# Turning the keys of groups 0 and 1 on TensorE, and query group 0 behind the last values of batch 0

## The chip, the cores and the metric

The kernel runs on one core of one Trainium2 chip. The metric is the time on the device in microseconds (us), median over runs; lower is better. TensorE (PE in the profile) multiplies matrices and writes to PSUM; VectorE (DVE), ScalarE (ACT) and GpSimd (POOL) work on tiles; SyncE (SP) issues most of the transfers.

## The reference, cut to what matters

Agent attention over four batches, followed by a feed-forward layer that takes the maximum of three products:

```python
# q, k, v: (4, 12544, 128); agents: (4, 49, 128)
def sm(a, b):                                   # softmax of scaled scores
    s = scale * (a @ b.transpose(0, 2, 1))
    s = s - s.max(-1, keepdims=True)
    e = np.exp(s)
    return e / (e.sum(-1, keepdims=True) + 1e-09)
agent_v = sm(agents, k) @ v                     # (4, 49, 128): all keys of a batch
x = (sm(q, agents) @ agent_v).reshape(50176, 128)
h = np.maximum(np.maximum(x @ w1, x @ w2), x @ w3)   # (50176, 768)
out = h @ w_out                                 # (50176, 128)
```

`agent_v` of a batch needs every key and value of that batch, and no query of the batch can be finished before it is there.

## The kernel before: the parts concerned

The kernel first goes through all keys and values of batch 0 (12 groups, called "early"). Then 49 query groups of 1024 rows follow. While the query groups of one batch are worked on, the keys and values of the next batch are taken along, one key group `s` of up to 1152 rows with each query group `s`. Instructions are not issued where they are written: each step is put in a list with a key, and the list is emitted in order of the keys. A step with a lower key stands earlier on its engine.

Matmuls contract over partitions, so keys and queries must first be turned (transposed) so that their 128 features lie on partitions. There are two ways in the kernel for this: on TensorE against an identity, into PSUM, with a copy to SBUF behind it, or by a DMA that transposes from SBUF to SBUF.

```python
def k_group(b, t0, n, key, s):          # n blocks of 128 keys; s is None for batch 0
    early = s is None
    ...
    def cast_k():                       # fp32 -> bf16 on GpSimd
        d["kb"] = work.tile([P, KT, C], BF16, tag="k_bf", bufs=3, name="k_bf")
        nc.gpsimd.tensor_copy(out=d["kb"][:, :n, :], in_=d["k"][:, :n, :])

    def turn_k():
        d["kT"] = work.tile([P, KT, P], BF16, tag="kT", bufs=3, name="kT")
        if early or s == 0:
            t = d["kT_ps"] = uv_tile(BF16).rearrange("p i c -> p (i c)")
            for j in range(n):
                nc.tensor.transpose(t[:, j * P:(j + 1) * P], d["kb"][:, j, :], ident)
        else:
            nc.sync.dma_start_transpose(out=d["kT"][:, :n, :],
                                        in_=d["kb"][:, :n, :].rearrange("p j c -> p (j c)"))

    def evacuate():
        nc.vector.tensor_copy(out=d["kT"][:, :n, :].rearrange("p j c -> p (j c)"),
                              in_=d["kT_ps"][:, :n * P])

    def scores(): ...                   # L255: kT x agents
    def exps(): ...                     # L260: e_k, on ScalarE
    def values(): ...                   # L266: v x e_k (and L269: sums, in batch 0)
    def add_values(): ...               # L276: into Vacc, on VectorE
```

`uv_tile` gives one of three PSUM buffers, which the hidden matmuls of the feed-forward layer use as well; whoever takes one waits until its last user of three takes ago is read out.

Once batch 0's values are summed, `k_tail` normalises them (`avT`) and multiplies them into the weights, which gives `G`, the product of the agents' values with the first layer, in two halves. The early version is cut here to its core:

```python
def product(c0, c1, on_vector):
    t = uv_tile()
    ...                                          # L352: avT x wall
    if on_vector:
        nc.vector.tensor_copy(out=G[b][:, c0:c1], in_=src)
    else:
        nc.scalar.activation(G[b][:, c0:c1], src, AF.Copy)
...
for i, (c0, c1) in enumerate(((C31, WC), (C21, C31))):    # 1024 and 768 columns
    on_vector = s is None and i == 1
```

A query group is turned (L415), copied (L419), scored (L429) and exponentiated (L435). Then come six pairs of hidden matmuls (L455): each first half `u` gets a ReLU on ScalarE (L470; the fourth goes L467, L478), each second half `v` is taken to the maximum with it on VectorE (L480). The output matmuls are L485 and L494, the scaling of the output L501. `keep_busy` (L200) and `fill` (L577) are matmuls whose results are not used; they keep TensorE occupied.

```python
if s == 0:
    at(last_key - 29.9, load)
    at(last_key - 3.5, cast)
    at(last_key + 0.63, turn_q, ("qt", 0), (), "om", [("qe", 0)])
    at(last_key + 0.635, evacuate, ("qe", 0), [("qt", 0)])
    at(last_key + 0.82, scores, ("s", 0), [("qe", 0)], "om", [("ex", 0)])
    at(last_key + 0.825, exps, ("ex", 0), [("s", 0)])
```

Of the kernel before, what the change touches and what calls it, by code (L numbers as in the profile page):

```python
# [11 lines left out]
AF = mybir.ActivationFunctionType  # L12
# [4 lines left out]
def kernel(  # L17
# [18 lines left out]
    nc = tc.nc  # L36
# [53 lines left out]
    def at(key, fn, name=None, needs=(), ring=None, frees=()):  # L90

        ops.append((key, len(ops), fn, name, needs, ring, frees))
# [115 lines left out]
    def k_group(b, t0, n, key, s):  # L210

        d = {}
        early = s is None

        def load():
            for name, src in (("k", k), ("v", v)):
                t = d[name] = load_tile()
                nc.sync.dma_start(t[:, :n, :], src[b, t0 * P:(t0 + n) * P, :].rearrange(
                    "(p j) c -> p j c", j=n))

        def cast_k():
            d["kb"] = work.tile([P, KT, C], BF16, tag="k_bf", bufs=3, name="k_bf")
            nc.gpsimd.tensor_copy(out=d["kb"][:, :n, :], in_=d["k"][:, :n, :])  # L223

        def cast_v():
            d["vb"] = work.tile([P, KT, C], BF16, tag="v_bf", bufs=4, name="v_bf")
            if early:
                nc.scalar.activation(d["vb"][:, :n, :], d["v"][:, :n, :], AF.Copy)  # L228
            else:
                nc.gpsimd.tensor_copy(out=d["vb"][:, :n, :], in_=d["v"][:, :n, :])  # L230

        def turn_k():
            d["kT"] = work.tile([P, KT, P], BF16, tag="kT", bufs=3, name="kT")
            if early or s == 0:
                t = d["kT_ps"] = uv_tile(BF16).rearrange("p i c -> p (i c)")
                for j in range(n):
                    nc.tensor.transpose(t[:, j * P:(j + 1) * P], d["kb"][:, j, :], ident)  # L237
# [8 lines that stand above are left out]
        def scores():  # L246
            if early:
                d["pair"] = uv_tile()
                d["s"] = d["pair"][:, 0, :]
                last_tile["t"] = d["s"]  # L250
            else:
                d["s"] = host[s]
            t = d["s"]
            for j in range(n):
                nc.tensor.matmul(t[:, j * A:(j + 1) * A], d["kT"][:, j, :], agT[:, b, :A],  # L255
                                 start=(j == 0), stop=True, skip_group_check=True)

        def exps():
            d["e"] = work.tile([P, KT * A], BF16, tag="e_k", bufs=3, name="e_k")
            nc.scalar.activation(d["e"][:, :n * A], d["s"][:, :n * A], AF.Exp, scale=scale)  # L260

        def values():
            t, c = (d["pair"][:, 1, :], 0) if early else (d["s"], CV)
            for j in range(n):
                e = d["e"][:, j * A:(j + 1) * A]
                nc.tensor.matmul(t[:, c:c + A], d["vb"][:, j, :], e, start=(early and j == 0),  # L266
                                 stop=True, skip_group_check=True)
                if early:
                    nc.tensor.matmul(t[:, A:2 * A], ones_bf, e, start=False, stop=True,  # L269
                                     skip_group_check=True)  # L270

        def add_values():
            w = 2 * A if early else A
            src = d["pair"][:, 1, :w] if early else d["s"][:, CV:CV + A]
            if t0:
                nc.vector.tensor_tensor(out=Vacc[b], in0=src, in1=Vacc[b], op=ALU.add)  # L276
            else:
                Vacc[b] = work.tile([P, w], FP32, tag=f"Vacc{w}", name="Vacc")
                nc.vector.tensor_copy(out=Vacc[b], in_=src)

        def add_exps():
            if t0:
                nc.gpsimd.tensor_tensor(out=Eacc[b][:, :n * A], in0=Eacc[b][:, :n * A],  # L283
                                        in1=d["e"][:, :n * A], op=ALU.add)
            else:
                Eacc[b] = work.tile([P, KT * A], FP32, tag="Eacc", name="Eacc")
                nc.gpsimd.tensor_copy(out=Eacc[b], in_=d["e"])

        if early:
            g = ("early", t0)  # L290
            at(key - 30, load)
            at(key - 5, cast_k)
            at(key - 4, cast_v)
            at(key, turn_k, ("kt", g), (), "uv", [("kt_out", g)])
            at(key + 0.5, evacuate, ("kt_out", g), [("kt", g)])

            last = [("normalise", 0)] if t0 + n == NT else []
            late = max(0, (key - last_key) / 6 + 2)
            at(min(key + 6.6, last_key + 0.58 + 0.02 * late), scores, ("ks", g), [("kt_out", g)],
               "uv", [("ka", g)] + last)  # L300
            at(min(key + 7, last_key + 0.64 + 0.01 * late), exps, ("ke", g), [("ks", g)])
            done = last_key + (0.6 + 0.1 * late if late >= 1 else 0.55)
            at(min(key + 13.2, done), values, ("kv", g), [("ke", g)])
            at(min(key + 13.6, done + 0.01), add_values, ("ka", g), [("kv", g)])
        else:
            at(key + KEY["ks"] - 22, load)
            at(max(key + KEY["ks"] - 10, last_key - 3.4), cast_k)
            at(max(key + KEY["ks"] - 8, last_key - 3.3), cast_v)
            if s:
                at(max(key + KEY["ks"] - 6.5, last_key - 3.2), turn_k, ("kt_out", s))  # L310
            else:
                at(last_key + 1.05, turn_k, ("kt", s), (), "uv", [("kt_out", s)])
                at(last_key + 1.06, evacuate, ("kt_out", s), [("kt", s)])

            at(key + KEY["ks"] if s else KEY["u0"] + 0.6, scores, ("ks", s), [("kt_out", s), ("ho", s)])
            at(key + KEY["ke"], exps, ("ke", s), [("ks", s)])
            at(key + KEY["ke"] + 1.5, add_exps, ("kx", s), [("ke", s)])
            at(key + KEY["kv"], values, ("kv", s), [("ke", s)])
            at(key + KEY["ka"], add_values, ("ka", s), [("kv", s)])

    def k_tail(b, sum_key, keys, s):
        d = {}
# [41 lines left out]
        at(sum_key + (0.9 if s is None else 0.01), normalise, ("normalise", b),  # L364
           [("ka", ("early", NT - last_size)) if s is None else ("total", s)])
        for i, (c0, c1) in enumerate(((C31, WC), (C21, C31))):
            on_vector = s is None and i == 1
            at(keys[i], lambda c0=c0, c1=c1, on_vector=on_vector: product(c0, c1, on_vector),
               ("product", b, i), [("normalise", b)], "uv", [("product", b, i)])

# [12 lines left out]
    def q_group(s):  # L383
        pairs = [range(0, 2), range(2, 4)]
        n, nh = GT, GT // 2
        parts = split(s * GT, (s + 1) * GT, 2)
        key = 6.0 * s
        d = {}
# [27 lines left out]

        def evacuate():
            d["qT"] = work.tile([P, GT, P], BF16, tag="qT", bufs=3, name="qT")
            nc.vector.tensor_copy(out=d["qT"].rearrange("p j c -> p (j c)"), in_=d["qT_ps"])  # L419

        def turn_q_dma():
            d["qT"] = work.tile([P, GT, P], BF16, tag="qT", bufs=3, name="qT")
# [95 lines left out]
        if s == 0:  # L518
            at(last_key - 29.9, load)
            at(last_key - 3.5, cast)  # L520
            at(last_key + 0.63, turn_q, ("qt", 0), (), "om", [("qe", 0)])
            at(last_key + 0.635, evacuate, ("qe", 0), [("qt", 0)])
            at(last_key + 0.82, scores, ("s", 0), [("qe", 0)], "om", [("ex", 0)])
            at(last_key + 0.825, exps, ("ex", 0), [("s", 0)])
        elif s < SB:
            at(key + K["qt"] - 20, load)
            at(max(key + K["qt"] - 7, last_key - 3), cast)
            put("qt", turn_q, ring="om", frees=[("qe", s)])
            put("qe", evacuate, ("qt", s), *([("s", s - 3)] if s >= 3 else []))
        else:  # L530
            at(key + K["s"] - 24, load)
            at(key + K["s"] - 8, cast)
            at(key + K["s"] - 5.5, turn_q_dma, ("qe", s))
# [48 lines left out]
    last_key = KEY["u0"] - 2  # L582
# [7 lines left out]
    fillers = []  # L590
    for g, n in enumerate(first_sizes):
        k_group(0, sum(first_sizes[:g]), n, first_key + 6.0 * g, None)

        if 4 <= g < len(first_sizes) - 5:
            fillers += [(first_key + 6.0 * g + 0.55, 3), (first_key + 6.0 * g + 1.3, 3)]
    k_tail(0, last_key, (last_key + 0.95, last_key + 0.96), None)
    for key, n in fillers + [(last_key + 0.9, 2), (last_key + 1.1, 3)]:
        at(key, lambda n=n: keep_busy(n), ("busy", key), (), "om", [("busy", key)])
    tails = {b * NT // GT: b for b in range(1, B)}
    hosting = set()  # L600
# [44 lines left out]
```

The softmax here doesn't subtract the row's maximum and nothing guards it: scores larger than these inputs give would overflow.

## Time and profile before

| what | before |
|---|---|
| time, median of 3 runs | 473.62 us (472.06 to 474.02) |
| span of the profiled execution | 473.2 us |
| TensorE busy | 439.0 us (93%) |
| VectorE busy | 408.1 us (86%) |
| ScalarE busy | 395.9 us (84%) |
| GpSimd busy | 166.1 us (35%) |
| mean granted TensorE clock | 0.991 |
| transfers | 118.04 MB, mean 249 GB/s |

Busy time says how full an engine is over the whole span; it does not say which engine another one waits for in a given stretch. For that there are the chain of work that ended last, which is followed back from the last instruction, the waits, and the timeline with the idle time ahead of each instruction and the instruction that ended it. Stretches of the span can be tabled one by one with each engine's busy time, the granted TensorE clock as a share of full speed, and the busy share of the 16 DMA engines. Matmuls overlap in time, so their busy time in a table of stretches is not the same as the time between their starts.

### The profile page before, as it was taken

How to read it: one execution, taken by the hardware profiler on the slowest of the kernel's cores; microseconds unless marked ns; L12 is line 12 of the kernel's file. 1: busy time of each engine (PE TensorE's matmuls, PEld its weight loads, DVE VectorE, ACT ScalarE, POOL GpSimd, SP SyncE). 2: the span in 40 equal slices, each digit the busy share in tenths (PEclk: the TensorE clock that was granted, in tenths of full speed). 3: DMA queues.
4: the chain of work that ended last, by engine and by line, in shares of the span. 5: the costliest groups of instructions: out<-in, count | busy, mean ns of one | idle time of the engine just before them, and what ended most of it. 6: DMA issues, size and time to landing. Idle time of an engine off the chain costs nothing.

```text
span 473.2 us, 13322 instructions
## 1 busy us (share of the span) xinstructions
PE 439.0 (93%) x5470; PEld 273.4 (58%) x5470; DVE 408.1 (86%) x519; ACT 395.9 (84%) x460; POOL 166.1 (35%) x166
## 2 busy tenths in 40 slices
PE   2497799999998999999999999999989999999996
PEld 2365256666665666666655766666655555555554
DVE  3165569999998999999998999999998999999995
ACT  3365668998888989889898899898989999999992
POOL 3244736455252364553460645535130011110000
PEclk9999979999999999999999999999999999999999
DMA  8999999998977999996987999985554767463412
GB/s 326 394 413 405 348 347 336 258 322 206 305 283 237 270 333 277 323 279 199 326 274 255 293 281 306 310 255 157 160 112 123 209 171 197 146 162 89 113 74 106
DMA packets 80648, 118.04 MB, mean 249 GB/s; under 512 B 54407, under 2 KB 55883, under 8 KB 80587
## 3 DMA queue, kind: packets, MB, share of 16 engines
q1 hardware_dynamic: 80384, 117.10, 80.2%
q8 instruction: 42, 0.69, 0.6%
q14 instruction: 19, 0.16, 0.1%
q10 hardware_dynamic: 203, 0.10, 0.1%
HBM read 78.74 MB, written 25.69 MB: 221 GB/s over the span
## 4 chain that ended last, share of the span: by engine, by line
PE 76%; DMA 12%; DVE 7%; ACT 3%; issue 2%; POOL 0%; SPq 0%; DVEq 0%; ACTq 0%; POOLq 0%
PE uv_ps L455 32%; PE o_ps L494 27%; DMA st<-in_k_dram 7%; PE o_ps L485 5%; DVE r L480 5%; PE m_ps L415 4%; PE m_ps L429 3%; DMA wst<-in_moe_w_dram 2%; DMA kT<-k_bf 2%; ACT a_sb L470 2%; PE m_ps L255 1%; PE m_ps L266 1%; DVE o_sb L501 1%; DMA ag_st<-in_agents_dram 1%; PE m_ps L443 1%
## 5 line engine op out<-in xcount | busy, mean ns | idle before, releaser
L480 DVE TENSOR_TENSOR r<-uv_ps,a_sb 128x1024 bf16<-128x1024 f32 x245 | 297.4, 1220 | 19.2 <-PE uv_ps L455 11.0
L470 ACT ACTIVATE a_sb<-uv_ps 128x1024 bf16<-128x1024 f32 x245 | 241.2, 1027 | 12.1 <-PE uv_ps L455 11.6
L455 PE MATMUL uv_ps<-e_q,G 49*128 49x512 bf16 (+3 forms) x1248 | 186.4, 370 | 5.2 <-DVE r L480 3.1
L494 PE MATMUL o_ps<-wo_bf,r 128*128 128x128 bf16 x2352 | 176.4, 220 | 0.0
L494 PEld LDWEIGHTS <-r 128*128 128x128 bf16 x2352 | 137.6, 98 | 44.1 <-issue 42.7
L455 PEld LDWEIGHTS <-G 49*128 49x128 bf16 x1248 | 56.1, 94 | 66.9 <-issue 31.9
L283 POOL TENSOR_TENSOR Eacc<-Eacc,e_k 128x441 f32<-128x441 f32 (+1 forms) x30 | 30.5, 1016 | 133.7 <-ACT e_k L260 133.7
L501 DVE TENSOR_TENSOR o_sb<-o_ps,recips 128x512 f32<-128x512 f32 x98 | 67.6, 690 | 9.8 <-PE o_ps L494 7.0
L410 POOL CAST q_bf<-st 128x1024 bf16<-128x1024 f32 x49 | 51.1, 1042 | 70.3 <-DMA qT<-q_bf 68.5
L478 ACT ACTIVATE r<-uv_ps 128x1024 bf16<-128x1024 f32 x49 | 50.2, 1024 | 26.4 <-PE uv_ps L455 26.4
L223 POOL CAST k_bf<-st 128x1152 bf16<-128x1152 f32 (+2 forms) x45 | 50.6, 1124 | 31.2 <-DMA st<-in_k_dram 24.2
L467 ACT ACTIVATE uv_ps<-uv_ps 128x1024 f32<-128x1024 f32 x49 | 49.6, 1013 | 1.9 <-PE uv_ps L455 1.9
L485 PE MATMUL o_ps<-G,e_q 128*128 128x256 bf16 x196 | 38.0, 276 | 1.8 <-DVE o_sb L501 1.8
L230 POOL CAST v_bf<-st 128x1152 bf16<-128x1152 f32 (+1 forms) x33 | 37.5, 1136 | 0.5 <-DMA st<-in_v_dram 0.5
L435 ACT ACTIVATE e_q<-m_ps 128x512 bf16<-128x512 f32 x49 | 29.8, 609 | 2.5 <-PE m_ps L429 2.5
L419 DVE COPY qT<-m_ps 128x1024 bf16<-128x1024 bf16 x36 | 24.5, 680 | 1.8 <-PE m_ps L415 1.7
L415 PEld LDWEIGHTS <-q_bf 128*128 128x128 bf16 x288 | 16.6, 99 | 15.4 <-issue 12.6
L228 ACT ACTIVATE v_bf<-st 128x1152 bf16<-128x1152 f32 (+1 forms) x12 | 12.9, 1072 | 14.4 <-DMA st<-in_v_dram 14.4
L485 PEld LDWEIGHTS <-e_q 128*128 128x128 bf16 x196 | 12.9, 98 | 20.6 <-issue 20.6
L415 PE MATMUL m_ps<-ident,q_bf 128*128 128x128 bf16 x288 | 22.7, 222 | 1.1 <-POOL q_bf L410 1.1
L243 DVE COPY kT<-uv_ps 128x1152 bf16<-128x1152 bf16 (+1 forms) x13 | 9.2, 705 | 16.2 <-PE uv_ps L237 16.2
L260 ACT ACTIVATE e_k<-m_ps 128x441 bf16<-128x441 f32 (+1 forms) x33 | 19.1, 578 | 3.5 <-PE m_ps L255 3.5
(67 smaller groups left out, 224.9 us busy)
## 6 DMA issues: line engine op xcount, KB each, us to landing
st<-in_q_dram SPq DMA_DIRECT2D x46, 512.0 KB, 4.6
out_dram<-o_sb SPq DMA_DIRECT2D x46, 512.0 KB, 3.5
st<-in_k_dram SPq DMA_DIRECT2D x40, 576.0 KB, 6.5
st<-in_v_dram SPq DMA_DIRECT2D x40, 576.0 KB, 7.1
st<-in_k_dram SPq DMA_DIRECT2D x3, 512.0 KB, 4.6
st<-in_v_dram SPq DMA_DIRECT2D x3, 512.0 KB, 5.6
wst<-in_moe_w_dram SPq DMA_DIRECT2D x3, 384.0 KB, 10.4
st<-in_q_dram SPq DMA_DIRECT2D x2, 384.0 KB, 4.1
```

The source lines that it names most:

```text
L223: nc.gpsimd.tensor_copy(out=d["kb"][:, :n, :], in_=d["k"][:, :n, :])
L230: nc.gpsimd.tensor_copy(out=d["vb"][:, :n, :], in_=d["v"][:, :n, :])
L410: nc.gpsimd.tensor_copy(out=d["qb"], in_=d["q"])
L415: nc.tensor.transpose(t[:, j * P:(j + 1) * P], d["qb"][:, j, :], ident)
L455: nc.tensor.matmul(t[:, h, j0 * P:j1 * P], G[b][h * H:h * H + A, col + f * P:col + (f + 1) * P], d["e"][h * H:h * H + A, j0 * P:j1 * P], s ...
L467: nc.scalar.activation(u, u, AF.Relu)
L470: nc.scalar.activation(a_sb[f], u, AF.Relu)
L478: nc.scalar.activation(r, v_ps[f], AF.Relu)
L480: nc.vector.tensor_tensor(out=r, in0=v_ps[f], in1=a_sb[f], op=ALU.max)
L485: nc.tensor.matmul(t[:, i * 2 * C:(i + 1) * 2 * C], d["e"][:, jj * P:(jj + 1) * P], G[batch[jj]][:, C1O:C1O + 2 * C], start=(i == 0), stop ...
L494: nc.tensor.matmul(t[:, c:c + C], r_sb[f][:, h, jj * P:(jj + 1) * P], wo_bf[:, f, :], start=False, stop=True, skip_group_check=True)
L501: nc.vector.tensor_tensor(out=d["out"][:, j:j + m, :], in0=d["o", o].rearrange("p (j c) -> p j c", c=C), in1=d["r"][:, j:j + m].unsqueeze( ...
```

## The change

It does four things around the switch from the keys of batch 0 to the first query groups:

1. The keys of group 1 are turned on TensorE, like those of group 0, in place of the DMA transpose. The copy out of PSUM is on VectorE.
2. Query group 0 is turned behind the last values of batch 0 and no longer ahead of them, so that the values, which `G` needs, don't stand behind the queries. Its copy goes to ScalarE; its scores and exponential come later, between the two halves of the product.
3. The two halves of `G` change engines: the first (1024 columns) is copied by VectorE, the second (768 columns) by ScalarE.
4. One filler matmul less stands behind the product.

On TensorE the order in the changed kernel is: last values of batch 0, query turning, two fillers, first half of the product, scores of query 0, second half of the product, keys of group 0, two fillers, hidden matmuls. The keys of group 1 come after the second half of the fourth hidden pair of query group 0. On VectorE their copy stands ahead of the copy of query group 1.

```diff
         def turn_k():
             d["kT"] = work.tile([P, KT, P], BF16, tag="kT", bufs=3, name="kT")
-            if early or s == 0:
+            if early or s < 2:
@@ key groups
-            if s:
+            if s > 1:
                 at(max(key + KEY["ks"] - 6.5, last_key - 3.2), turn_k, ("kt_out", s))
             else:
-                at(last_key + 1.05, turn_k, ("kt", s), (), "uv", [("kt_out", s)])
-                at(last_key + 1.06, evacuate, ("kt_out", s), [("kt", s)])
+
+                turn = 1.2 if s else last_key + 1.05
+                at(turn, turn_k, ("kt", s), (), "uv", [("kt_out", s)])
+                at(turn + 0.05, evacuate, ("kt_out", s), [("kt", s)])
@@ product
-            on_vector = s is None and i == 1
+            on_vector = s is None and i == 0
@@ query groups
         def evacuate():
             d["qT"] = work.tile([P, GT, P], BF16, tag="qT", bufs=3, name="qT")
-            nc.vector.tensor_copy(out=d["qT"].rearrange("p j c -> p (j c)"), in_=d["qT_ps"])
+            if s:
+                nc.vector.tensor_copy(out=d["qT"].rearrange("p j c -> p (j c)"), in_=d["qT_ps"])
+            else:
+                nc.scalar.activation(d["qT"].rearrange("p j c -> p (j c)"), d["qT_ps"], AF.Copy)
@@ query group 0
-            at(last_key + 0.63, turn_q, ("qt", 0), (), "om", [("qe", 0)])
-            at(last_key + 0.635, evacuate, ("qe", 0), [("qt", 0)])
-            at(last_key + 0.82, scores, ("s", 0), [("qe", 0)], "om", [("ex", 0)])
-            at(last_key + 0.825, exps, ("ex", 0), [("s", 0)])
+            at(last_key + 0.82, turn_q, ("qt", 0), (), "om", [("qe", 0)])
+            at(last_key + 0.825, evacuate, ("qe", 0), [("qt", 0)])
+            at(last_key + 1, scores, ("s", 0), [("qe", 0)], "om", [("ex", 0)])
+            at(last_key + 1.01, exps, ("ex", 0), [("s", 0)])
@@ the tail of batch 0 and the fillers
-    k_tail(0, last_key, (last_key + 0.95, last_key + 0.96), None)
-    for key, n in fillers + [(last_key + 0.9, 2), (last_key + 1.1, 3)]:
+    k_tail(0, last_key, (last_key + 0.95, last_key + 1.02), None)
+    for key, n in fillers + [(last_key + 0.9, 2), (last_key + 1.1, 2)]:
```

## The prediction

> **What bounds the kernel now.** I first read the busy shares. TensorE is busy 93% of the span, VectorE 86%, ScalarE 84%, so in most of the kernel the three share one rhythm: from 70 us on, the score matmuls of successive key groups start at 69.49, 77.84, 86.19 and 94.54 us, 8.35 us apart, and the waits from 64 to 130 us hold nothing on a DMA for TensorE. The change touches none of that. It touches 41 to 65 us, so the chain of work that ended last comes next, for the first 64 us (start, duration, what):
>
> ```profile
> 38.57 9.04 DMA st<-in_k_dram
> ...
> 47.73 1.15 POOL k_bf L223
> 48.88 0.03 POOL q_bf L410
> 48.91 9.40 DMA kT<-k_bf
> 58.30 0.05 issue
> 58.35 0.55 PE m_ps L255 x9
> ```
>
> The reader is to see who holds the path: until 47.6 us loads of keys, then one cast on GpSimd, and then a single transfer, the DMA transpose of the keys of group 1, for 9.40 us. TensorE takes over only at 58.35. The timeline shows how long TensorE stood for it (start, duration, engine, line, what, then in brackets the idle time before and who ended it):
>
> ```profile
> 53.70 0.39 PE L455 MATMUL uv_ps<-e_q,G 49*128 49x512 bf16 x2
> ...
> 55.91 0.39 PE L577 MATMUL o_ps<-busy,ident 128*128 128x512 bf16 x1
> 58.35 0.55 PE L255 MATMUL m_ps<-agT,kT 128*128 128x49 bf16 x9 [2.05 <-DMA kT<-k_bf]
> ```
>
> The wait itself is 2.05 us. It has a second price, which the table of stretches shows (stretch, length, busy time of PE, PEld, DVE, ACT, POOL, granted TensorE clock, DMA share, GB/s):
>
> ```profile
> 40.95:44.36 3.41, 1.94 (x53) 1.76 (x51) 1.42 (x4) 0.80 (x3) 2.02 (x2) 1.00 1.02 407
> ...
> 54.60:58.01 3.41, 1.51 (x9) 0.41 (x7) 2.45 (x2) 2.34 (x4) 1.01 (x2) 1.00 1.33 221
> 58.01:61.43 3.42, 3.08 (x18) 0.92 (x19) 1.02 (x1) 1.21 (x2) 2.94 (x3) 0.50 1.00 400
> 61.43:64.84 3.41, 3.41 (x29) 1.95 (x28) 1.66 (x4) 1.73 (x3) 2.38 (x3) 0.50 1.09 371
> ```
>
> Right behind the stretch with 1.51 us of TensorE work, the clock is 0.50 for two stretches, 6.83 us. Hence group 1 to group 2 takes 69.49 - 58.35 = 11.14 us, and group 0 to group 1 58.35 - 48.36 = 9.99, against 8.35 later, although these early groups have less output work.
>
> The second place is the switch from batch 0's keys to its first queries, in the timeline around 43 us:
>
> ```profile
> 41.73 0.57 ACT L260 ACTIVATE e_k<-uv_ps 128x196 bf16<-128x196 f32 x2 [0.55 <-PE uv_ps L255]
> 42.97 0.62 PE L415 MATMUL m_ps<-ident,q_bf 128*128 128x128 bf16 x8 [1.10 <-POOL q_bf L410]
> 43.63 0.69 DVE L419 COPY qT<-m_ps 128x1024 bf16<-128x1024 bf16 x1 [1.73 <-PE m_ps L415]
> 44.24 0.64 DVE L276 TENSOR_TENSOR Vacc<-uv_ps,Vacc 128x98 f32<-128x98 f32 x2
> 45.68 0.95 PE L352 MATMUL uv_ps<-wall,avT 128*64 128x512 bf16 x10 [0.37 <-DVE avT L340]
> ```
>
> The exponentials are ready at 42.30, but the values behind them start only at 43.37, because the turning of query group 0 stands ahead of them on TensorE and waits 1.10 us for the cast of its queries (42.91). Its copy of 0.69 us then stands ahead of the two sums on VectorE as well.
>
> **What the Trainium skill says.** "VectorE: DVE Perf Modes", The three transpose paths, gives 390 ns for one 128x128 bf16 block on TensorE, result in PSUM, and 1309 ns on the DMA crossbar. The trace goes the same way: nine blocks took 9.40 us by DMA here (median of all 32 such transposes 4.8, least 3.8, issue to landing), while the nine of group 0 took 0.68 us on TensorE plus a 0.74 us copy. "DMA: Bandwidth & Descriptors", Issuing engines are not separate DMA queues, says that all DMAs run on the same 16 engines and interleave; this agrees with the slow landing, as the DMA share around the issue is 1.02 to 1.04. "TensorE: Matmul & The Clock Gate", Part 1, says the clock halves after an idle window of about 3.4 us and that the windows run freely; the trace has the half clock and stretches of 3.41 us, but 1.51 us of the window before was busy, so less than a full idle window was enough. "VectorE: DVE Perf Modes", Why PSUM operands drop a tier, says fp32 from PSUM runs at the 1x rate; the 128x768 copy of G at 0.96 us and the 128x1024 maximum at 1.22 fit that, so I take 1.22 us for the 128x1024 copy of G, which moves to VectorE.
>
> **Part 1, the switch (query group 0).** Values first: they can start at about 42.06, and the second eight at 42.35 behind the second exponential. The eight pairs issue in some 0.2 us and end at 42.72 (before 43.99). The two sums are then done at about 43.1 instead of 44.88; reciprocal to product took 45.68 - 44.91 = 0.77, so the product could start at 43.9 (before 45.68). On TensorE in between are the query turning, 42.97 to 43.42, still tied to the cast, and two fillers of 0.21, so it is free at about 43.85. Gain so far 1.8 us.
> Then, for the first half of G: 43.9 + 0.67 (product to copy, as before) = 44.57, plus 1.22 on VectorE = 45.8. ScalarE: copy of the queries 43.63 to 44.65 (1.02, as its other 1024-wide ones; VectorE took 0.69), scores at 44.7, exponential 45.15 to 45.63, second half of G (0.80) to 46.43. TensorE: second product to 45.3, keys of group 0 to 45.8, two fillers to 46.25. The hidden matmuls start at 46.25 (before 47.82). Keys copied 46.0 to 46.7, second hidden pair behind 46.43, scores of group 0 at 46.9 instead of 48.36: 1.5 us gained.
> Most of it is lost at the next data: turning query group 1 needs its cast, which ends at 49.86 and hangs on the load that landed at 47.61. This does not move. TensorE gets there at about 49.3 and waits; the turning starts at 49.9 instead of 50.68. **0.8 us is left.**
>
> **Part 2, keys of group 1 on TensorE.** Cast by 48.88, they are turned behind the hidden pairs, at 51.4 to 51.9 (9 x 0.053, with the 0.68 us of group 0 as the measure including latency). This adds on VectorE a copy of 0.65 us (start to start), and the order of instructions puts it ahead of the copy of queries 1 and of the maximum r1, which must free a PSUM buffer: copy 52.1, queries 52.75, r1 53.35 to 54.57. The hidden pair that in the trace stands at 53.70 then starts only at 54.63; the added work costs more than part 1 had left, and TensorE is 0.9 us behind.
> After that: its ReLU to 56.05, scores of query 1, two pairs, one filler, and the key scores of group 1 at 57.0, with nothing to wait for, instead of 58.35: **+1.35 us.** From there at full clock: ScalarE one ReLU to 57.6 and the exponential to 58.1, VectorE the maximum of 1.2 to 58.1, three hidden pairs to 59.05, three fillers to 59.7, values at 59.7 against 62.34: **+2.64 us in all.** Before, half clock lasts until 64.84: from the values to the run of 20 output matmuls took 66.07 - 62.34 = 3.73 us, a group later 74.43 - 71.66 = 2.77; that is **0.96 us** more. Sum 3.6 us. From there it is the same instructions in the same order, bound by TensorE, VectorE and ScalarE, so all of it should reach the end: 473.62 - 3.6 = 470.0; I say 470.1.
>
> **Rivals.** (a) The clock drops anyway. With the hand-worked times TensorE idles about 0.9 us before 54.6 and 0.4 before 52.55. For it: the changed code takes one filler off TensorE, and the nine transposes are not the dense work of a filler. Against it: busy time of that stretch comes to some 2.5 us, and 40.95 to 44.36 with 1.94 kept its clock. If it happens, the 6.83 us at half rate return and about 2 to 2.5 us are lost: 472.
> (b) The next DMA transpose takes the place of the one removed. Group 2's landed at 55.24 + 8.2 = 63.4 for a use at 69.49. In the changed kernel the use comes at about 65.9, while the issue, after its cast (53.03), is no longer queued behind another transpose; I expect it in by 62. If it lands late by 1 to 2 us, 471 to 472.
> (c) The dearer start on VectorE is milder than worked out, and part 1 keeps more: up to 4.5 us gained, 469.
> (d) It is hidden: later transfers can't come earlier, and the kernel ends as before. Against it: behind 64 us no TensorE wait on a DMA is left, and the key transposes land 4.7 us after an issue at 73.09 for a use at 86.19, with about 8 us to spare.
>
> **Range and chances.** The step with most doubt is the walk from 50 to 57 us, in which each engine waits for another; I give it 1 us either way, and the spread of before is 2 us (472.06 to 474.02). Eight in ten: 468.5 to 472.3. Faster by over 2% would need below 464.2, 9.5 us, more than the wait, the half clock and the switch together: 2%. Slower by over 2% would need a stall of 9.5 us that nothing shows: 1%. Within 2%: 97%.
>
> **What would show it.** Right: no DMA transpose in the chain near 49 to 58 us; no TensorE wait for kT; granted clock 1.00 from 58 to 65; key scores of group 0, 1 and 2 at about 46.9, 57.0 and 65.9; a wait of TensorE near 49.5 for the cast of queries 1; the VectorE copies of kT and queries back to back near 52 to 53.4. Wrong: a stretch at clock 0.50 elsewhere in 45 to 70, group 2's keys on the chain, or a distance between key scores that stays above 8.35 us after group 2.

## The result

The changed kernel takes 470.18 us (median of 4 runs, 469.35 to 470.29); the kernel before takes 472.91 us beside it. The ratio is 0.9937 with a 95% interval of 0.9909 to 0.9965. A later series gave 469.98 us against 473.93 us and a ratio of 0.9921 (0.9903 to 0.9939). So the change saves between 2.7 and 4 us of some 473, less than 2%.

### The profile page after: what moved, and what is told of

It reads as the page before. It is cut to its first block, busy times and chain, and to the rows that moved or that the text cites. A ratio compares the mean times of both kernels' runs of the same rounds, so it can differ in the third digit from the quotient of the medians.

```text
span 467.5 us, 13338 instructions
## 1 busy us (share of the span) xinstructions
PE 437.3 (94%) x5478; PEld 273.4 (58%) x5478; DVE 408.3 (87%) x519; ACT 396.7 (85%) x461; POOL 165.8 (35%) x166
## 4 chain that ended last, share of the span: by engine, by line
PE 78%; DMA 10%; DVE 6%; ACT 3%; issue 1%; POOL 0%; SPq 0%; DVEq 0%; ACTq 0%; POOLq 0%
PE uv_ps L460 33%; PE o_ps L499 28%; DMA st<-in_k_dram 7%; PE o_ps L490 6%; DVE r L485 4%; PE m_ps L417 4%; PE m_ps L434 3%; DMA wst<-in_moe_w_dram 2%; ACT a_sb L475 2%; PE m_ps L266 1%; PE m_ps L255 1%; DVE o_sb L506 1%; DMA ag_st<-in_agents_dram 1%; PE m_ps L448 1%; PE uv_ps L354 1%
## 5 line engine op out<-in xcount | busy, mean ns | idle before, releaser
L237 PE MATMUL uv_ps<-ident,k_bf 128*128 128x128 bf16 x116 | 11.7, 262 | 10.8 <-POOL k_bf L223 10.8
```

## The profile after

The chain of work that ended last, of the changed kernel, around the place where the DMA transpose stood (start, duration, what):

```profile
38.61 8.98 DMA st<-in_k_dram
...
47.71 1.15 POOL k_bf L223
48.86 0.99 POOL q_bf L412
...
49.90 0.62 PE m_ps L417 x8
...
51.38 1.03 ACT r L483
...
54.68 0.83 DVE r L485
...
55.82 1.22 DVE r L485
...
57.48 0.75 PE o_ps L582 x3
```

The loads still hold the path until 47.6 us, to within 0.02 us of before. Behind them the 9.40 us of `kT<-k_bf` are gone; short steps on GpSimd, TensorE, ScalarE and VectorE follow each other instead. The chain names the step that came last at each place, not by how much: the cast at 48.86 is on it by less than 0.1 us, as a run below shows.

From TensorE's timeline of the changed kernel, the lines that matter here (start, duration, engine, line, what, idle time before and who ended it):

```profile
43.01 0.62 PE L417 MATMUL m_ps<-ident,q_bf 128*128 128x128 bf16 x8 [0.26 <-POOL q_bf L412]
44.08 0.63 PE L354 MATMUL uv_ps<-wall,avT 128*64 128x512 bf16 x6
46.98 0.40 PE L255 MATMUL m_ps<-agT,kT 128*128 128x49 bf16 x9
49.90 0.62 PE L417 MATMUL m_ps<-ident,q_bf 128*128 128x128 bf16 x8 [0.53 <-POOL q_bf L412]
51.21 0.68 PE L237 MATMUL uv_ps<-ident,k_bf 128*128 128x128 bf16 x9
53.53 0.39 PE L460 MATMUL uv_ps<-e_q,G 49*128 49x512 bf16 x2
55.60 0.39 PE L255 MATMUL m_ps<-agT,kT 128*128 128x49 bf16 x9
64.19 0.39 PE L255 MATMUL m_ps<-agT,kT 128*128 128x49 bf16 x9
```

The three L255 lines are the key scores of groups 0, 1 and 2. The wait for `kT` is gone. From group 2 on the distance is 8.35 us, as before, and what is gained at group 2 is kept to the end: the two profiled spans are 473.2 and 467.5 us.

The stretches of the changed kernel (columns as before: PE, PEld, DVE, ACT, POOL, granted clock, DMA share, GB/s):

```profile
54.60:58.01 3.41, 3.28 (x27) 1.32 (x27) 3.33 (x3) 3.30 (x6) 3.01 (x3) 1.00 1.03 412
58.01:61.43 3.42, 3.42 (x51) 2.24 (x49) 2.89 (x6) 2.63 (x4) 3.29 (x4) 1.00 1.22 218
61.43:64.84 3.41, 3.37 (x45) 1.89 (x42) 3.04 (x4) 3.41 (x6) 0.00 (x0) 1.00 1.09 399
```

Where TensorE was busy for 1.51 us before, it now is for 3.28, and the clock is 1.00 in both stretches where it was 0.50.

| start of the key scores, us | before | predicted | changed | gained |
|---|---|---|---|---|
| group 0 | 48.36 | 46.9 | 46.98 | 1.38 |
| group 1 | 58.35 | 57.0 | 55.60 | 2.75 |
| group 2 | 69.49 | 65.9 | 64.19 | 5.30 |

The profiled executions thus differ by 5.3 us at group 2, more than the medians do (2.7 to 4 us). An experiment was needed for that as well: how much of it is the half clock, and does every execution have it?

## The experiments

### Part 1 alone

```diff
-            if early or s < 2:
+            if early or s == 0:
...
-            if s > 1:
+            if s:
```

> Part 1 alone: query group 0 behind the last values, copy on ScalarE, halves of G swapped, one filler less; the keys of group 1 are turned by DMA as before. Theory A (the gain is the wait for the DMA-turned keys of group 1 and the half clock behind it): key scores of group 0 at about 47.0 us as in the changed kernel, those of group 1 still at 58.3, the wait for kT longer (about 3.4 us instead of 2.05), group 2 no earlier than 69; time as before, within 0.5 us. Theory B (the gain is the earlier switch): group 2 some 1.4 us earlier than in the kernel before, time 1.4 us lower. Theory C (the gain is DMA traffic taken away): as before.

473.63 us against 473.87; ratio 0.9998 (0.9983 to 1.0013). TensorE's timeline:

```profile
47.00 0.40 PE L255 MATMUL m_ps<-agT,kT 128*128 128x49 bf16 x9
58.15 0.56 PE L255 MATMUL m_ps<-agT,kT 128*128 128x49 bf16 x9 [3.21 <-DMA kT<-k_bf]
```

Group 0 comes as early as in the changed kernel, and nearly the whole lead of 1.4 us turns into a longer wait at group 1: 3.21 us instead of 2.05. (Group 1 comes 0.2 us earlier only because the transfer's result does.) In this profiled execution the half clock began inside that wait, so that part of it fell on idle time, and group 2 came at 68.53, before the 69 that I had expected; over 14 timed runs no gain is left. By itself the earlier switch, with the filler that goes with it, is worth nothing: Theory B falls. That filler was not run alone.

### Part 2 alone

```diff
-        if early or s == 0:          # kernel before
+        if early or s < 2:
...
+                turn = 1.2 if s else last_key + 1.05     # group 1: turned on TensorE
```

> Part 2 alone: keys of group 1 turned on TensorE, the switch as before. Theory A: key scores of group 0 at 48.4, group 1 at about 56.3 with no wait for kT, clock 1.00 from 58 to 65, group 2 at about 64.9; time 0.5 to 0.8 us above the changed kernel, so about 2 us below the kernel before. Theory B: time as before. Theory C: time as the changed kernel.

472.06 us against 473.87; ratio 0.9961 (0.9949 to 0.9973), 1.8 us saved. Key scores at 48.36, 56.91 and 65.81, no wait for `kT`, clock 1.00 from 58 to 65. That part 2 takes away the wait and the half clock is as Theory A says; but my number for the rest was wrong. The changed kernel is not 0.5 to 0.8 us ahead of this one but 1.9 us (472.06 to 470.2, or to the 470.21 that the kernel with the unused transfer, below, took in this same series), and the marks say why: its lead is 1.38 us at group 0, 1.31 at group 1 and 1.62 at group 2. With the wait gone, the lead of the earlier switch reaches the end whole. The two parts are not additive: 0 alone, 1.8 alone, 2.7 to 4 together.

### The clock kept, the wait left

```diff
         def scores():
...
+            if s == 1:
+                for _ in range(10):
+                    fill()           # kernel before, 10 unused matmuls ahead of group 1's scores
```

> The kernel before with ten filler matmuls (0.215 us each, 2.15 us) on TensorE ahead of the key scores of group 1, where it waits for the DMA: the wait for the keys stays, only the idle time is filled. Theory A with the half clock as a share of its own: group 1 still at about 58.4, clock 1.00 from 58 to 65, group 2 at 58.4 + 8.6 = 67.0 instead of 69.5; time up to 2.5 us lower than before, less if the executions that are timed did not all drop the clock. If the half clock costs nothing: group 2 at 69.5, time as before or 0.1 us more.

```profile
54.60:58.01 3.41, 3.22 (x19) 1.20 (x18) 2.45 (x2) 2.90 (x4) 1.33 (x2) 1.00 1.31 215
58.01:61.43 3.42, 3.42 (x39) 1.61 (x38) 1.23 (x1) 1.72 (x3) 2.60 (x3) 1.00 1.01 394
61.43:64.84 3.41, 3.26 (x42) 2.00 (x40) 3.19 (x5) 2.63 (x3) 2.73 (x3) 1.00 1.13 385
```

Columns as above. The clock stays at 1.00, group 1 stands at 58.86 (in this execution group 0 was already 0.56 us later than before), group 2 at 67.45: the distance is 8.59 us, exactly that of the changed kernel, against 11.14 before. So in the profiled execution the half clock was worth 2.55 us. That the idle time was its cause shows in the timed executions as well: 19 of 22 have a mean clock of 0.998 or more here, 9 of 48 in the kernel before, in the same series. (A drop in the last two microseconds alone, as in the changed kernel's first profile, leaves a mean of 0.998.) Yet over 22 timed runs the kernel saves only 0.8 us: 473.11 against 473.87, ratio 0.9986 (0.9975 to 0.9998). Span and mean clock of each timed execution, over all series, say why:

| executions of | mean clock 0.998 and above | below 0.998 |
|---|---|---|
| kernel before (67) | 10, mean span 470.7 us | 57, mean span 472.3 us |
| changed kernel (9) | 5, mean span 467.8 us | 4, mean span 468.6 us |

An execution of the kernel before with a lowered clock is 1.6 us longer on average, not 2.55; ten of 67 don't pay it. The ten fillers are not free either: where the clock is kept, their kernel's spans are 471.1 us on average against 470.7 (why is not shown). Between the executions with the clock kept, the kernels before and after differ by 470.7 - 467.8 = 2.9 us, close to the 2.75 us that the marks show at group 1, where the half clock has hardly begun. Over all executions the mean spans are 472.1 and 468.2 us. Of these 3.9 us about 1.0 belong to the clock: (472.1 - 470.7) - (468.2 - 467.8). With nine executions of the changed kernel, this split is rough.

### The transfer left in, unused

```diff
+            if s == 1:
+                at(max(key + KEY["ks"] - 6.5, last_key - 3.2), turn_unused)   # DMA transpose of
+                                                  # group 1's keys into a tile nobody reads
```

> The changed kernel, and in addition the DMA transpose of the keys of group 1 into a tile that nobody reads, issued where the kernel before issues it. Theory C (what helps is that this transfer no longer loads the DMA engines and SyncE's queue): the gain goes, time about 472.9. Theory A: trace as the changed kernel with group 2 within 0.5 us of 64.2, time within 0.5 us of 470.2. If the next DMA transpose is the hidden limit, group 2's keys land after 65 and TensorE waits for them.

470.21 us; ratio 0.9926 (0.9902 to 0.995). SyncE's timeline shows that the transfer and what stands behind it in the queue are as before the change:

```profile
48.80 1.35 SPq L244 DMA_TRANSPOSE kT_unused<-k_bf  x1
50.20 3.87 SPq L415 DMA_DIRECT2D st<-in_q_dram  x1
...
55.20 4.24 SPq L239 DMA_TRANSPOSE kT<-k_bf  x1
```

It lands after 9.4 us, as before. Group 2's scores stand at 64.19 with no wait. As traffic the transfer costs nothing that shows here; it cost because TensorE needed its result. Theory C falls. Rival (b) of the prediction does not come true either, but it is near: queued behind that transfer, group 2's keys land 8.9 us after 55.20, at 64.1, just ahead of their use at 64.19.

### The cast of query group 1 ahead of the keys

```diff
-            at(max(key + K["qt"] - 7, last_key - 3), cast)
+            at(last_key - 3.215 if s == 1 else max(key + K["qt"] - 7, last_key - 3), cast)
```

> The changed kernel with the GpSimd cast of query group 1 ahead of that of the keys of group 1, in GpSimd's idle time before 47.7: TensorE's wait of 0.53 us for that cast goes. Prediction's step (this wait takes away most of what the earlier switch had gained): group 1 and 2 about 0.5 us earlier, time 0.5 us lower than the changed kernel. Rival (the ReLUs on ScalarE from 47.91 on carry the lead, and the wait lies beside them): group 1 within 0.15 us of 55.60, group 2 within 0.15 us of 64.19, time as the changed kernel. If the cast of the queries has to wait for their load, the keys of group 1 are cast later than 48.86, and nothing is gained.

```profile
46.97 0.40 PE L255 MATMUL m_ps<-agT,kT 128*128 128x49 bf16 x9
49.29 0.62 PE L417 MATMUL m_ps<-ident,q_bf 128*128 128x128 bf16 x8
55.51 0.39 PE L255 MATMUL m_ps<-agT,kT 128*128 128x49 bf16 x9
64.10 0.39 PE L255 MATMUL m_ps<-agT,kT 128*128 128x49 bf16 x9
```

The turning of query group 1 comes 0.61 us earlier and waits for nothing, and the key scores move by 0.09 us. 470.12 us, ratio 0.9908 (0.9889 to 0.9928), as the changed kernel. All but 0.09 us of the wait of 0.53 lay beside the path. The chain of this run says what is next to come last: in place of the cast and the turning, it goes through two ScalarE steps from 48.92 to 50.76 us. So what carries the lead is ScalarE; its timeline in the changed kernel, and then in the one with part 2 alone:

```profile
47.91 1.94 ACT L475 ACTIVATE a_sb<-uv_ps 128x1024 bf16<-128x1024 f32 x2
49.72 1.05 ACT L472 ACTIVATE uv_ps<-uv_ps 128x1024 f32<-128x1024 f32 x1
51.38 1.02 ACT L483 ACTIVATE r<-uv_ps 128x1024 bf16<-128x1024 f32 x1 [0.61 <-PE uv_ps L460]
```

```profile
49.29 1.94 ACT L471 ACTIVATE a_sb<-uv_ps 128x1024 bf16<-128x1024 f32 x2
51.10 1.05 ACT L468 ACTIVATE uv_ps<-uv_ps 128x1024 f32<-128x1024 f32 x1
52.69 1.02 ACT L479 ACTIVATE r<-uv_ps 128x1024 bf16<-128x1024 f32 x1 [0.54 <-PE uv_ps L456]
```

The first two lines keep a lead of 1.38 us; of that, 0.07 is lost at the third, as long as TensorE waits for the cast. The cast itself could move, since only its place behind the cast of the keys held it: in this run it starts at 46.03 instead of 48.80. The prediction had it fixed.

### The order of the two VectorE copies

```diff
-                at(turn + 0.05, evacuate, ("kt_out", s), [("kt", s)])
+                at(turn + (0.1 if s else 0.05), evacuate, ("kt_out", s), [("kt", s)])
```

> The changed kernel with the two VectorE copies in the other order: queries of group 1 first, then the keys of group 1. Prediction's step (the key copy ahead of the query copy and of the maximum r1 holds a PSUM buffer, 0.9 us): group 1's key scores would come earlier. What the trace of the changed kernel says (the hidden pair at 53.53 takes the buffer that the keys themselves leave, and does not wait for r1): no gain; the pair that follows the keys' buffer starts up to 0.3 us later, group 2 within 0.4 us of 64.2, time within 0.5 us of the changed kernel.

469.49 us; ratio 0.9906 (0.9877 to 0.9934), as the changed kernel. Its profiled execution had the half clock for 3.41 us from 50.5 on, so its marks up to group 1 can't be compared; the distance from group 1 to group 2 is 8.60. In the changed kernel's own timeline the step falls more clearly. The hidden pair that I had put behind the end of r1 starts at 53.53, while VectorE's timeline has r1 still at work:

```profile
51.92 0.76 DVE L243 COPY kT<-uv_ps 128x1152 bf16<-128x1152 bf16 x1 [1.45 <-PE uv_ps L237]
52.60 0.68 DVE L422 COPY qT<-m_ps 128x1024 bf16<-128x1024 bf16 x1
53.19 1.22 DVE L485 TENSOR_TENSOR r<-uv_ps,a_sb 128x1024 bf16<-128x1024 f32 x1
```

r1 ends at 54.41. The pair can't have waited for it; it uses a buffer read out earlier, by elimination the one whose copy into `kT` ended at 52.68. I had taken the three buffers in strict turn, as the account of the kernel says; the trace does not bear that out.

### Query copy on VectorE; halves of G back

```diff
-            if s:
+            if True:                 # group 0's queries too are copied by VectorE
                 nc.vector.tensor_copy(out=d["qT"].rearrange("p j c -> p (j c)"), in_=d["qT_ps"])
```

> The changed kernel with the copy of query group 0 back on VectorE; the order puts it between the two sums and the reciprocal there. Theory: the reciprocal waits for the copy (ends at 44.3 instead of being free at 43.3), product 0.95 us later at 45.0, key scores of group 0 at about 47.9, group 1 at 56.5, group 2 at 65.1; time 0.7 to 1.0 us above the changed kernel. Rival (the switch doesn't reach the end, as its lead is lost at the cast of query group 1): group 1 within 0.2 us of 55.60, time as the changed kernel.

470.67 us; ratio 0.9937 (0.9917 to 0.9956), 0.7 us above the changed kernel in the same series, though the two intervals overlap. Product at 45.10 instead of 44.08, key scores at 47.78, 56.32 and 65.22, that is 0.80, 0.72 and 1.03 us late. The delay at the switch is still there at group 2, once more against my 0.8 us.

```diff
-            on_vector = s is None and i == 0
+            on_vector = s is None and i == 1
```

> The changed kernel with the halves of G on their former engines (first 1024 columns on ScalarE, last 768 on VectorE). Theory: ScalarE then does queries' copy, first half, exponential one after the other, the exponential ending near 46.2 instead of 45.7, while VectorE has its half done by about 46.5 and the keys' copy by 47.2: key scores of group 0 at about 47.3 instead of 46.98, all behind it 0.3 us later, time 0.1 to 0.4 us above the changed kernel. If the swap is worth nothing: within 0.1 us of 46.98.

470.36 us; ratio 0.9928 (0.9909 to 0.9947). From product to key scores of group 0 it takes 47.66 - 44.56 = 3.10 us, against 46.98 - 44.08 = 2.90. The swap is worth 0.2 us in the trace; the timed difference of 0.4 us is within the spread.

### The fillers

```diff
     def fill():
+        return                       # all 12 unused matmuls of the first two groups left out
```

> The changed kernel without any of the twelve filler matmuls that stand in the places of the output matmuls during query groups 0 and 1 (they compute nothing that is used). Theory A1 (fillers lie on the path of the first two groups, as the chain of the changed kernel has 0.22, 0.75, 0.32 and 0.75 us of them): key scores of group 1 0.3 to 0.6 us earlier than 55.60, of group 2 0.8 to 1.5 us earlier than 64.19; time about 469. Theory A2 (ScalarE and VectorE set the pace of these groups and the fillers only fill): group 2 within 0.3 us of 64.2. If TensorE then does too little, the clock drops to 0.50 for 6.83 us within 50 to 65 and up to 2.5 us are lost: time about 472.

471.0 us (468.69 to 472.48); ratio 0.9932 (0.9909 to 0.9955). Stretches:

```profile
47.77:51.19 3.42, 2.19 (x30) 1.14 (x27) 1.41 (x3) 3.27 (x4) 3.21 (x4) 1.00 1.04 415
51.19:54.60 3.41, 2.90 (x15) 1.29 (x15) 1.62 (x3) 1.96 (x3) 3.41 (x5) 0.51 1.02 405
```

The clock halves for 13.65 us in the profiled execution. Six of seven executions had a mean clock of 0.993 or less, with spans of 468.6 to 470.7 us; the one that kept it (0.999) had 466.9, shorter than any of the changed kernel (467.5 at least). Both Theory A1 and its price are there: the fillers cost time on the path, though one execution alone says so here, and without them the clock takes back what they cost: by the ratio the time is as the changed kernel's.

```diff
-                at(key - 6, fill, ...
+                at(key - 6, (lambda: None) if o and i >= 3 else fill, ...   # 3 of 12 left out
```

> The changed kernel without the last three ramp fillers alone, those ahead of the values of group 1 (57.41 to 58.07 in the changed kernel's trace). Theory A1: the values of group 1 start at 57.4 instead of 58.07, the output scale and the maximum behind them 0.3 to 0.6 us earlier, group 2 at about 63.7; clock stays 1.00; time about 0.4 us lower than the changed kernel. Theory A2: group 2 within 0.15 us of 64.2.

470.47 us; ratio 0.9915 (0.9893 to 0.9938). Group 1 to group 2 takes 65.54 - 57.20 = 8.34 us instead of 8.59, so those three were on the path with 0.25 us. But the profiled execution dropped its clock for 3.41 us from 51.05 on, behind a wait of 0.70 us for the cast of query group 1, ahead of the place where the fillers are missing. The time is as the changed kernel.

### Both small steps together

The earlier cast takes away idle time near 49.5 us, and three fillers fewer shorten the path behind it: the diffs of the cast and of the three fillers together.

> The changed kernel with both small steps: the cast of query group 1 ahead of the keys of group 1 on GpSimd (takes TensorE's idle time near 49.5 away), and without the three fillers ahead of the values of group 1. If the idle time near 49.5 is what lets the clock drop in some executions, the clock stays at 1.00 in nearly all of them here, and the 0.25 us of the shorter way from group 1 to group 2 (8.34 instead of 8.59 us) shows: time 0.2 to 0.5 us below the changed kernel. Rival: the fillers are needed to hold the clock in any case; then it drops in about half the executions and the time is as the changed kernel or up to 0.5 us above.

> The changed kernel once more, for how often its clock drops and for comparison within one series. Theory: the time is 470.2 within 0.4, its executions with clock at or above 0.998 at a span near 467.9 us; the kernel before beside it has spans of about 470.6 where the clock stays and 472.2 where it drops, so that about 2.9 us of the gain don't depend on the clock and the rest is the half clock that fewer executions have.

469.14 us (469.07 to 469.47), ratio 0.9902 (0.9881 to 0.9923), against 469.98 us (469.32 to 470.81), ratio 0.9921 (0.9903 to 0.9939), for the changed kernel in the same series. All four executions of the combined kernel had a mean clock of 0.998 or more and spans of 467.0 to 467.4; the changed kernel's were 467.5 to 469.0, at 0.994 to 1.0. Distances of 8.54 and 8.33 us between the key scores against 8.62 and 8.59 give 0.34 us, more even than the 0.25 us that I had counted on. That the rest is the clock is likely but not shown: the earlier cast alone also kept it at 0.998 or more in all four executions, with spans of 467.8 to 468.6 us, no shorter than the changed kernel's. The gain is 0.8 us by the medians; the intervals of the two ratios overlap, so its size is not settled, but its executions' spans lie wholly below those of the changed kernel, if by 0.1 us at the nearest. This is the fastest of the kernels run. The changed kernel's profiled execution in this series had its own half clock, for 3.41 us to 42.6 us, at the end of batch 0's keys.

## Why the prediction was right

The size was right, 3.6 us predicted and 2.7 to 4 us measured, and so was what bounds: the one wait for the DMA-turned keys, the half clock behind it, and nothing in traffic or in later transfers. That the sum came out was partly luck: it gave 1.35 us to the wait and the switch and 2.25 us to the clock, the runs about 2.9 and 1.0, and the two errors cancelled.

- **Part 1, up to group 0.** Right: product predicted at 43.9, measured 44.08; key scores 46.9 against 46.98. The order of steps on ScalarE and VectorE was as worked out.
- **"0.8 us is left."** Right for TensorE's turning of query group 1 and wrong for what follows. TensorE waited 0.53 us for the cast and started at 49.90, 0.78 us ahead of the kernel before, as foretold. But not all of a wait in the timeline is a wait on the path. The branch through ScalarE's ReLUs came less than 0.1 us earlier, and the lead stayed 1.3 us and more (part 2 alone against the changed kernel; the earlier cast).
- **"The hidden pair ... starts only at 54.63."** Wrong by 1.1 us: 53.53, since it did not need r1's buffer and the lead was larger. The keys' turning is not free. With part 1 alone, which turns nothing, the scores of query group 1 stand at 53.30 and in the changed kernel at 54.49; but that 1.2 us stands in place of a wait of 3.21.
- **Group 1.** +1.35 us predicted, +2.75 measured. The 1.1 us at the pair is one half the lead (1.31 us kept instead of 0.8) and one half a cheaper turning: the pair stands at 54.84 with part 2 alone, 1.1 us behind the kernel before, where the prediction charged 1.7 (from 0.8 ahead to 0.9 behind). The other 0.3 us is a shorter walk from the pair to the key scores, 2.07 us instead of 2.37.
- **The half clock.** In the prediction it was inside the step from 1.35 to 2.64 us and the last 0.96, 2.25 us together; in the profiled execution it was 2.55 (distance 11.14 against 8.59). The mistake was to charge every execution with it: over the timed executions it is about 1.0 us of the difference, since 1.6 us is its mean price in the kernel before, some don't have it, and the changed kernel has a little of it too.
- **Rivals.** (a), a drop in the changed kernel: four of its nine executions have a lower mean clock, at a price of 0.8 us and not of 2 to 2.5. In the one of them that was profiled the drop lies at 39.2 to 42.6 us, not behind the idle time that (a) names; where it lies in the others is not known. (b) did not happen, with less to spare than expected: group 2's keys took 10.0 us from an issue at 53.03, in at 63.0 and not by 62, for a use at 64.19. (d) did not happen. (c), a milder start on VectorE and a lead kept, was the truer reading of the mechanism; its 4.5 us is above what the timed runs show, because it left the clock's share as it was.

## What to carry to other kernels

Shortening what stands ahead of a wait for a transfer bought nothing here until the wait was gone, and then nearly all of it at once; measure such parts together. A wait in an engine's timeline, even one that the chain runs through, counts only by what it exceeds the next branch that meets it, so follow the other branches, here through ScalarE, before a wait is charged to the sum. One profiled execution overstates what a lowered clock costs when other executions don't have it, so compare span and mean clock over the timed executions.

## What was not expected of the hardware

The clock fell to 0.50 after stretches in which TensorE was far from idle. In the 3.41 us ahead of each drop it was busy for 1.32 us (changed kernel, second series), 1.51 (before), 1.90 (three fillers left out), 2.06 (part 1 alone), 2.13 (no fillers) and 2.26 us (order of copies), and in three of these (1.90, 2.13 and 2.26) no single gap was above 0.7 us. Yet two stretches kept the clock with 1.94 us of work and a gap of 1.1 us (40.95 to 44.36 of the kernel before) and with 2.15 us and a gap of 0.9 (35.87 to 39.28 of the changed kernel). So no single amount of busy time and no single length of gap, at least as these stretches cut it, separates the two, and which activity counts stays open. The drops lasted 3.41, 6.83 or 13.65 us, that is one, two or four times the same length. The Trainium skill's "TensorE: Matmul & The Clock Gate", Part 1, gives that length for its window and says that it runs freely, which fits drops that differ from one execution of a kernel to the next. It also puts a drop behind at least one idle window; here no window ahead of a drop was idle, and the measurement decides.
